# Gate rows behind the first score gather, a change of bank roles before the v products, and a later third band set in group 2: a fused attention and gMLP kernel

## The chip, the cores and the metric

The kernel runs on one core of one Trainium2 chip. The metric is device microseconds (us) of one execution, as the median of several; the profile is of one further execution. Engines: PE is the matmul engine (PEld its weight load), DVE the vector engine, ACT the scalar engine, POOL the general one, SP the engine whose queue issues nearly all transfers here. PSUM is the memory that PE writes; the kernel uses it as eight banks.

Before the change the time was 650.78 us (median of 3 runs, 650.62 to 651.17).

## The reference

The output is `g * a + (1 - g) * b`: a dilated sliding-window attention (32 heads of 32 columns, each token looks at itself and 7 earlier ones, 2 apart), a gMLP block, and a sigmoid gate per token.

```python
x = A_x                                        # 1 x 2048 x 1024
g = sigmoid((x * gate_w).sum(-1, keepdims=True))
# a: attention
qkv = x @ wqkv                                 # 1024 x 3072
logits = einsum('bhsd,bhswd->bhsw', q, k[idx]) * scale   # idx = s - 2 w, w = 0..7
o = einsum('bhsw,bhswd->bhsd', softmax(logits), v[idx])
a = o @ wo
# b: gMLP
z = gelu(x @ w_in)                             # 1024 x 3584
z1, z2 = z[..., :1792], layernorm(z[..., 1792:])
b = (z1 * (w_sp @ z2 + b_sp)) @ w_out
# ... (return g * a + (1 - g) * b; the mask for positions before the first token is left out)
```

## The kernel before

The large products are done in quads of seven block products each (a fast matrix multiplication), which trade matmuls for sums on DVE and copies on ACT. The attention works on eight groups of four heads. For each group PE computes **band sets**: small products that hold the scores of blocks of tokens against their windows. ACT evicts a set from PSUM into a slot in SBUF, the on-chip memory that the engines read (the two large sets of a group take three slots in turn), SP stores it to a buffer in DRAM, and a **gather** reads the scores of a whole group back in another layout. From there DVE takes maxima, ACT the exponential, DVE the weights, the products with v, and their sums.

```python
band_slots = [reg(R_OFF + o, 7 * BR)... for o in (30208, 32196, 38848)]
...
vq_slots = [reg(R_OFF + 39360 + 2 * VH * r, 2 * VH).bitcast(F32) for r in range(2)]
```

The third band slot starts at 38848 and is 1988 long, so it overlaps the first of the `vq_slots`, which take the **share copies** of the v quads (below). Group 2 uses the slots in the order 38848, 30208 for its two large sets (sets 2 and 3).

```python
def band_blocks(g, first, step, n, pairs=None):
    ...
        st = band_slots[band_at[0] % 3]
        band_at[0] += 1
    ...                                            # PE: the small products (L355), into banks 4 to 7
    dst = st[:, 0:n, lo:KW, :]
    src = _sub_ap(psum_all, 4 * 512 + lo, [[KW, n], [1, KW - lo], [512, HG]])
    nc.scalar.copy(dst, src)                       # ACT: eviction (L363)
    ...
        stored[id(st)].append(dma(band_free[0], 0.1 * k, lambda ...: sync.dma_start(dst, src), landed))
```

The group's interleaving with a q/k quad, and the place of the three sets:

```python
BAND_AT = (1, 3, 6)

def among_bands(g, quad):
    x = 0
    for n in range(7):
        next(quad)
        step()
        if n + 1 in (BAND_AT if g != 2 else (1, 3, 5)):
            band_set(g, x)
            x += 1
            step()
```

Each side of PSUM has four banks, whose roles X, Y, Z, V rotate from quad to quad. The start of a v quad (line numbers of the profile of before: L420, L426):

```python
bank_roles = [banks[0:4], banks[4:8]]
...
X, Y, Z, V = bank_roles[side]
...                                    # product 1 into X
nc.scalar.copy(Y[:, n], X[:, n])       # L420: the seed copy, for product 3
...                                    # product 2 into V
share(vs, V[:, n])                     # L426: the share copy, into a vq_slot
```

Group 2 is followed by the v quads, with `mark` matmuls (L558) that write two banks which the band sets have used:

```python
if g == 2:
    first = v_quad(0)
    for _ in range(2):
        next(first)
        step()
    mark(bank_roles[1][1:3], VH)
    run(v_quad(1), first, step=step)
```

DVE's work, the transfers and the exponentials are ordered by a model inside the program (`clock`, `advance`), which plays the engines forward with estimated durations and issues whatever it finds ready first. An engine then runs its instructions in that order. Its start, and the queue after the gate:

```python
T_START = (0.0, 0.0, 0.0)
...
sync.dma_start(<g_d>, g_s[:])
gate_dma = sync.dma_start(<og_d>, omg_h[:])
...
band_data[0], band_free[0], v_data[0] = T_START
clock["SP"], clock["DMA"] = 0.5, 1.5
...
next_bands()                                       # the gather of group 0's scores
dma(0.0, 0.1, lambda: sync.dma_start(g_att[:], <g_d>))
next_v(1)
```

The sums of the attention, on DVE (the lines that an experiment below edits are these):

```python
for n, ws in enumerate(...):
    yield now, ..., lambda ...: tt(a, a, b, ALU.add), not n
yield now, 1.14, lambda: tt(p3[:, 0:2, :], p3[:, 0:2, :], p3[:, 2:4, :], ALU.add), True
```

Of the kernel before, what the change touches and what calls it, by code (L numbers as in the profile page):

```python
# [13 lines left out]
P = 128  # L14
# [9 lines left out]
NJ = 16  # L24
# [34 lines left out]
def kernel(  # L59
# [34 lines left out]
    g_d = dpool.tile([S], F32, name="g_d")  # L94
    og_d = dpool.tile([S], F16, name="og_d")
# [3 lines left out]
    g_s = sm.tile([16, P], F32, name="g_s")  # L99
# [5 lines left out]
    omg_h = sm.tile([16, P], F16, name="omg_h")  # L105
    g_att = sm.tile([P, NJ], F32, name="g_att")
# [91 lines left out]
    sync = _SyncProxy()  # L198
# [3 lines left out]
    clock = dict(PE=0.0, ACT=0.0, DVE=0.0, SP=0.0, DMA=0.0)  # L202
    live = [False]
    pinned = {}
# [31 lines left out]
    def pe(dur, ready=0.0):  # L236
        return take("PE", dur, ready)
# [9 lines left out]
    def act(dur, ready):  # L247
        if live[0]:
            advance(ready)
        return take("ACT", dur, ready)  # L250
# [6 lines left out]
    def dma(ready, dur, f, landed=None, timed=False):  # L257
        if not live[0]:
            return f()
        item = [ready, dur, f, landed, timed]  # L260
        due.append(item)
        return item
# [64 lines left out]
    for i in range(4):  # L327
        vp_tile(i, middle=None)
    band_at = [0]
    last_sub = [None]  # L330
    last_evac = [None]
    BAND_SETS = [(0, 8, 2), (1, 1, 7), (9, 1, 7)]

# [1 line left out]
    stored = {}  # L335

    def band_blocks(g, first, step, n, pairs=None):
        qt, kt_ = qT_slots[g % 2], kT_slots[g % 2]
        if first == 0:
            st = band0  # L340
        else:
            st = band_slots[band_at[0] % 3]
            band_at[0] += 1
        for item in stored.get(id(st), ()):
            issue(item)
        ready = pe(T_BAND * (0.3 if n < 3 else 1.0), band_free[0])
        lo = W - 1 if first == 0 else 0
        for m in range(n):
            e, b = divmod(first + m * step, 8) if pairs is None else (m // pairs, first + m % pairs)
            for q in range(2):  # L350
                skip = lo if q == 0 else 0
                at = P * b + QB * q
                for h in range(HG):
                    hp = slice(DH * h, DH * (h + 1))
                    nc.tensor.matmul(banks[4 + h][QB * q:QB * (q + 1), m * KW + skip:(m + 1) * KW], qt[hp, e, at:at + QB],  # L355
                                     kt_[hp, e, at - (W - 1) + skip:at + QB], start=True, stop=True,
                                     tile_position=(DH * h, QB * q), skip_group_check=True)
        band_free[0] = act(0.55 if n < 3 else 1.73, ready + 0.2) + 0.15
        if lo:
            nc.scalar.copy(st[QB:P, 0:n, 0:lo, :], _sub_ap(psum_all[QB:P, :], 4 * 512, [[KW, n], [1, lo], [512, HG]]))  # L360
        dst = st[:, 0:n, lo:KW, :]
        src = _sub_ap(psum_all, 4 * 512 + lo, [[KW, n], [1, KW - lo], [512, HG]])
        nc.scalar.copy(dst, src)  # L363
        bd = band_d[g]

        def landed(t):
            band_data[g] = max(band_data[g], t)

        stored[id(st)] = []
        for q in range(2):  # L370
            for e in range(1 if pairs is None else 2):
                k = n if pairs is None else pairs
                dst = bass.AP(tensor=bd.tensor, offset=bd.offset + (2 * first + 16 * e + q) * BS, ap=[[BR, QB], [2 * step * BS, k], [1, BR]])
                src = st[QB * q:QB * (q + 1), e * k:(e + 1) * k].rearrange("p m k h -> p m (k h)")
                stored[id(st)].append(dma(band_free[0], 0.1 * k, lambda dst=dst, src=src: sync.dma_start(dst, src), landed))

    def band_set(g, x):
        band_blocks(g, *BAND_SETS[x])
# [12 lines left out]
    bank_roles = [banks[0:4], banks[4:8]]  # L391
# [4 lines left out]
    last_store = [None]  # L396
# [170 lines left out]
    def v_quad(i):  # L567
        st = vst_slots[i % 4]
        vs = vq_slots[i % 2]

        def parts(m, a, *bs):
            d = st[:, a, :].rearrange("p (g d h) -> p g d h", g=GR, h=HG)
            full = slice(3 * m, 3 * m + 2)
            at, half, hs = (0, 256, slice(0, 2)) if m == 0 else (64, 0, slice(2, 4))
            yield [d[:, full]] + [b[:, at:at + 256].rearrange("p (g h d) -> p g d h", g=2, h=HG) for b in bs]
            yield [d[:, 2, :, hs]] + [b[:, half:half + 64].rearrange("p (h d) -> p d h", h=2) for b in bs]

        for item in stored.get(id(st), ()):
            issue(item)
        stored[id(st)] = []  # L580

        def store(a):
            dv = bass.AP(tensor=v_d.tensor, offset=v_d.offset + (GP * (S + 16) + 16 + (i + 8 * a) * P) * C, ap=[[C, P], [(S + 16) * C, GR], [1, C]])
            stored[id(st)].append(dma(max(clock["ACT"], clock["DVE"]), 0.92, lambda: sync.dma_start(dv, st[:, a, :].rearrange("p (g c) -> p g c", g=GR)), v_landed))

        def put(m, a, b):
            act(0.85, clock["PE"] + 0.2)
            for dst, src in parts(m, a, b):
                nc.scalar.copy(dst, src)
            if m:  # L590
                store(a)

        def put_sum(m, a, b):
            dve(0.75, clock["PE"] + 0.2)
            insts = [nc.vector.tensor_tensor(dst, src, v, ALU.add) for dst, src, v in parts(m, a, b, vs)]
            if not m:
                store(a)
            return insts[0]

        return strassen([wvr[0][:, k, :] for k in K4], [wvr[0][:, 4 + k, :] for k in K4], [wvr[1][:, 4 + k, :] for k in K4],  # L600
                        *[[wvs[q][:, k, :] for k in K4] for q in range(4)], *x_tiles(i), vs,
                        lambda X: put(0, 0, X), lambda Z: put_sum(0, 1, Z), lambda V: put(1, 0, V), lambda Y: put_sum(1, 1, Y),
                        N=VH, flip=True, turn=False)
# [222 lines left out]
    SQH = 8  # L826
    squares = [(n, x) for n in range(16) for x in range(2)]
    LEAN = (True, True)
    T_START = (0.0, 0.0, 0.0)

    def square(n, x, junk):
        c = slice(x * HF, (x + 1) * HF)
# [48 lines left out]
# [4 lines that stand above are left out]
        for n in range(7):  # L885
            next(quad)
            step()
            if n + 1 in (BAND_AT if g != 2 else (1, 3, 5)):
                band_set(g, x)
                x += 1  # L890
                step()
        bands_have[0] = g + 1
        next(quad, 0)
# [55 lines left out]
    def step():  # L949
        advance(clock["PE"])  # L950
# [44 lines left out]
    gate_mm = nc.tensor.matmul(glT, gl_s[:], ident32[:], start=True, stop=True)  # L995
    gate_act = nc.scalar.activation(omg[:], glT, ACT.Tanh, scale=0.5)
    nc.vector.tensor_scalar(g_s[:], omg[:], 0.5, 0.5, ALU.mult, ALU.add)
    gate_vec = nc.vector.tensor_scalar(omg_h[:], omg[:], -0.5, 0.5, ALU.mult, ALU.add)
    sync.dma_start(bass.AP(tensor=g_d.tensor, offset=g_d.offset, ap=[[P, 16], [1, P]]), g_s[:])
    gate_dma = sync.dma_start(bass.AP(tensor=og_d.tensor, offset=og_d.offset, ap=[[P, 16], [1, P]]), omg_h[:])  # L1000

    settle()
    live[0] = True
    for inst in (gate_mm, gate_act, gate_vec, gate_dma):
        pinned[inst.ins.engine] = inst.ins.name
    for x in clock:
        clock[x] = 0.0
    band_data[0], band_free[0], v_data[0] = T_START
    clock["SP"], clock["DMA"] = 0.5, 1.5
    stored.clear()  # L1010
    bands_have[0] = 1
    next_bands()
    dma(0.0, 0.1, lambda: sync.dma_start(g_att[:], bass.AP(tensor=g_d.tensor, offset=g_d.offset, ap=[[NJ, P], [1, NJ]])))
    next_v(1)
    def load_wvr():
        for m in range(2):
# [8 lines left out]
    for g in range(NG):  # L1025
        main = with_quads(g, group_tiles(g))
        if g in (1, 2, 3, 4):
            load_wqk_later(g + 3, clock["PE"])
        hold[0] = g == NG - 1
        paired = play_group(g)  # L1030
        if not paired:
            play(main[0:8 - (not g)])
        if g == 2:
            first = v_quad(0)
            for _ in range(2):
                next(first)
# [3 lines that stand above are left out]
            for i in range(2, 8, 2):  # L1040
                run(v_quad(i), v_quad(i + 1), step=step)
            advance(clock["PE"] + 1.0)
            v_have[0] = NG
            next_v()
            load_later(0, clock["PE"] + 4.0, 6.0)
        if not paired:
            play(main[8 - (not g):])
# [559 lines left out]
            load_act(fp // 2 - 1)  # L1607
    out_sums_late()
    traced[0] = len(nc.cur_bb.bb.instructions)
    pinned[gate_dma.ins.engine] = last_store[0].ins.name  # L1610
    for xa in ((1, 1), (0, 1), (0, 0), (1, 0)):
        load_block(1, *xa)
    act_sums(0)
# [46 lines left out]
```

## Time and profile before

| | before |
|---|---|
| time, median | 650.78 us |
| span of the profiled execution | 648.3 us |
| PE busy | 637.5 us (98%) |
| DVE busy | 519.3 us (80%) |
| ACT busy | 298.1 us (46%) |
| granted PE clock, 200 to 250 us | 1.00 |

How to read it: a PE that is busy 98% of the span leaves 10.8 us that could be won by taking away waits.

Because the start-up differs between executions, I give positions below from the start of the gate's own matmul (L995) where I say so; it lies at 44.45 us in the profile of before.

### The profile page before, as it was taken

To read this page: it belongs to the slowest core of one execution; us is meant where nothing else is said; L and a number is where in the kernel's file an instruction comes from. 1 tells how busy PE (TensorE), PEld (TensorE's weight loads), DVE (VectorE), ACT (ScalarE), POOL (GpSimd) and SP (SyncE) were. 2 spreads that over 40 slices of the span, in tenths; PEclk is the share of its full clock that TensorE was granted. 3 is DMA by queue.
4 is the path that set the end of the run, shared out by engine and by line. 5 is a ranking of instruction groups with operands and counts; after the bars stand their busy time and mean duration, and the time that the engine had idled before them with its cause. 6 is when DMAs were issued, how large, how long until landed. Compare 5 with 4: busy or idle time off the path is not lost.

```text
span 648.3 us, 11298 instructions
## 1 busy us (share of the span) xinstructions
PE 637.5 (98%) x4345; PEld 336.2 (52%) x4391; DVE 519.3 (80%) x816; ACT 298.1 (46%) x644; POOL 15.4 (2%) x27
## 2 busy tenths in 40 slices
PE   8999999999999999999999999999999999999997
PEld 4544467444455555444444444444444444868684
DVE  0347998999899999999988766987569999586852
ACT  3547677676786878799643121121121121202120
POOL 2210000000000000001000000000000000000000
PEclk9999999999999999999999999999999999999999
DMA  9979564798687012258994578369487383557501
GB/s 218 202 162 283 115 153 103 175 226 197 133 216 201 1 51 76 66 160 233 259 257 130 130 166 189 100 202 283 91 190 174 84 158 102 107 138 127 124 28 49
DMA packets 227174, 98.19 MB, mean 151 GB/s; under 512 B 174496, under 2 KB 214064, under 8 KB 227120
## 3 DMA queue, kind: packets, MB, share of 16 engines
q1 hardware_dynamic: 226256, 95.70, 61.2%
q0 software_dynamic: 576, 1.57, 0.9%
q8 instruction: 34, 0.56, 0.4%
q10 hardware_dynamic: 288, 0.20, 0.1%
q14 instruction: 20, 0.16, 0.1%
HBM read 44.31 MB, written 36.61 MB: 125 GB/s over the span
## 4 chain that ended last, share of the span: by engine, by line
PE 90%; ACT 4%; SPq 2%; DMA 1%; DVE 1%; issue 1%; DVEq 0%; ACTq 0%
PE psum_all L402 71%; PE psum_all L1484 8%; PE psum_all L293 6%; PE psum_all L303 2%; PE psum_all L355 2%; ACT arena L838 2%; ACT arena L1175 1%; PE psum_all L790 1%; SPq L178 1%; DMA arena<-in_A_wqkv_dram 1%; SPq L194 1%; ACT arena L363 1%; ACT arena L783 1%; DMA arena<-zg_d 1%; DVE psum_all L473 0%
## 5 line engine op out<-in xcount | busy, mean ns | idle before, releaser
L402 PE MATMUL psum_all<-arena 128*128 128x512 f16 (+6 forms) x2481 | 502.5, 362 | 3.3 <-issue 0.8
L402 PEld LDWEIGHTS <-arena 128*128 128x128 f16 (+1 forms) x2518 | 244.9, 98 | 253.4 <-issue 3.2
L676 DVE TENSOR_TENSOR arena<-arena,att_A 128x2048 f16<-128x2048 bf16 x64 | 75.5, 1220 | 0.3
L473 DVE TENSOR_TENSOR psum_all<-psum_all,arena 128x512 f32<-128x512 f32 (+1 forms) x78 | 51.0, 669 | 8.7 <-PE psum_all L402 5.7
L1484 PE MATMUL psum_all<-arena 128*128 128x256 f16 (+1 forms) x468 | 51.6, 273 | 0.0
L1484 PEld LDWEIGHTS <-arena 128*128 128x128 f16 x468 | 45.8, 98 | 5.5
L293 PE MATMUL psum_all<-arena 128*128 128x512 bf16 x183 | 42.0, 379 | 1.2 <-issue 0.8
L420 ACT COPY psum_all<-psum_all 128x512 f32<-128x512 f32 (+1 forms) x24 | 12.5, 519 | 66.2 <-PE psum_all L402 65.5
L783 ACT ACTIVATE arena<-psum_all 128x448 bf16<-128x448 f32 x64 | 34.2, 545 | 18.3 <-PE psum_all L402 9.0
L1175 ACT ACTIVATE arena<-psum_all 128x512 bf16<-128x512 f32 x56 | 31.4, 613 | 19.8 <-PE psum_all L402 9.0
L680 DVE TENSOR_TENSOR arena<-arena 128x2048 f16<-128x2048 f16 x32 | 37.9, 1218 | 0.0
L363 ACT CAST arena<-psum_all 128x1988 f16<-128x1988 f32 (+3 forms) x25 | 33.9, 1358 | 2.7 <-PE psum_all L355 2.3
L838 ACT ACTIVATE arena<-arena 128x896 bf16<-128x896 bf16 x32 | 30.9, 981 | 0.0
L545 DVE TENSOR_TENSOR arena<-arena 128x512 f16<-128x512 bf16 (+5 forms) x60 | 30.1, 534 | 0.4
L444 ACT COPY psum_all<-psum_all 128x512 f32<-128x512 f32 (+1 forms) x24 | 12.3, 518 | 37.5 <-PE psum_all L402 36.8
L293 PEld LDWEIGHTS <-arena 128*128 128x128 bf16 x192 | 18.1, 98 | 21.5 <-DMA arena<-in_A_wqkv_dram 0.6
L869 ACT CAST arena<-psum_all 128x512 bf16<-128x512 f32 x40 | 22.2, 592 | 12.4 <-DVE psum_all L473 9.8
L388 DVE TENSOR_TENSOR arena<-arena 128x2048 f16<-128x2048 bf16 x8 | 9.4, 1221 | 20.9 <-DMA arena<-in_A_x_dram 20.7
L486 ACT COPY psum_all<-psum_all 128x512 f32<-128x512 f32 (+1 forms) x39 | 21.7, 570 | 6.6 <-PE psum_all L402 6.0
L426 ACT COPY arena<-psum_all 128x512 f32<-128x512 f32 (+1 forms) x24 | 12.7, 533 | 26.1 <-PE psum_all L402 22.5
L431 ACT COPY psum_all<-psum_all 128x512 f32<-128x512 f32 (+1 forms) x24 | 12.4, 517 | 25.8 <-PE psum_all L402 24.8
L549 DVE TENSOR_TENSOR arena<-arena 128x1024 f16<-128x1024 f16 (+1 forms) x16 | 11.4, 715 | 15.7 <-PE psum_all L402 15.7
(113 smaller groups left out, 530.3 us busy)
## 6 DMA issues: line engine op xcount, KB each, us to landing
arena<-v_d SPq DMA_DIRECT2D x8, 960.0 KB, 5.8
z_d<-arena SPq DMA_DIRECT2D x14, 512.0 KB, 3.9
arena<-z_d SPq DMA_DIRECT2D x14, 512.0 KB, 4.4
zg_d<-arena SPq DMA_DIRECT2D x56, 128.0 KB, 2.2
arena<-zg_d SPq DMA_DIRECT2D x32, 224.0 KB, 3.2
band_d<-arena SPq DMA_DIRECT2D x28, 248.5 KB, 4.2
arena<-in_A_wqkv_dram SPq DMA_DIRECT2D x16, 256.0 KB, 4.2
o_d<-arena SPq DMA_DIRECT2D x4, 1024.0 KB, 5.7
```

Of the source, the lines that this page charges most:

```text
L293: nc.tensor.matmul(ps[:], w[:, t, kt, :], xT[:, kt, 512 * c:512 * (c + 1)], start=(kt == 0), stop=(kt == KT - 1))
L363: nc.scalar.copy(dst, src)
L402: nc.tensor.matmul(bank[:, 0:N], lhsT, rhs, start=(start and m == 0), stop=(m == n - 1), skip_group_check=True)
L473: last_add[0] = nc.vector.tensor_tensor(out[:, n], a[:, n], vs, ALU.add)
L545: return [lambda a=a: nc.vector.tensor_tensor(*a) for a in args]
L676: lambda ws=ws, in0=in0, in1=in1: tt(p5[:, ws], in0[:, ws], in1[:, ws], ALU.mult)), False
L680: lambda a=p3[:, ws], b=p3[:, ws.start + 4:ws.stop + 4]: tt(a, a, b, ALU.add)), not n
L783: nc.scalar.activation(z2[:, i + 8 * a, ZC * c:ZC * (c + 1)], bank[:, 0:ZC], ACT.Gelu_apprx_tanh, accum_out=s1[:, 4 * n + c:4 * n + c + 1])
L838: return nc.scalar.activation(junk, src, ACT.Square, accum_out=(s2, s2h)[x][:, n:n + 1])
L869: nc.scalar.copy((qT_slots, kT_slots)[t][g % 2][:, :, 256 * (c + 2 * x):256 * (c + 2 * x + 1)], bank[:].rearrange("p (n e) -> p e n", e=2))
L1175: last_gelu[0] = nc.scalar.activation(z1s[:, f, a, :], bank[:], ACT.Gelu_apprx_tanh)
L1484: nc.tensor.matmul(bank[:, h], l, r, start=(start and m == 0), stop=(m == len(ab) - 1), skip_group_check=True)
```

## The change

Its intent: let the gather of group 0's scores go as soon as the bands are stored, not after the gate rows; make the second v product write a bank that is free earlier; and give the third band set of group 2 the same place among the steps as the other groups have. The core of the diff:

```diff
-    last_sub = [None]
+    last_band = [None]
...
+        last_band[0] = stored[id(st)][-1]
...
-    T_START = (0.0, 0.0, 0.0)
+    T_START = (-1.0, 0.0, 3.0)
...
-            if n + 1 in (BAND_AT if g != 2 else (1, 3, 5)):
+            if n + 1 in BAND_AT:
...
-    sync.dma_start(<g_d>, g_s[:])
-    gate_dma = sync.dma_start(<og_d>, omg_h[:])
...
-    for inst in (gate_mm, gate_act, gate_vec, gate_dma):
+    for inst in (gate_mm, gate_act, gate_vec, last_band[0]):
...
-    clock["SP"], clock["DMA"] = 0.5, 1.5
+    clock["SP"], clock["DMA"] = -0.5, 0.0
...
     next_bands()
-    dma(0.0, 0.1, lambda: sync.dma_start(g_att[:], <g_d>))
+    dma(0.6, 0.1, lambda: sync.dma_start(<g_d>, g_s[:]))
+    dma(0.6, 0.1, lambda: sync.dma_start(<og_d>, omg_h[:]))
+    dma(0.6, 0.1, lambda: sync.dma_start(g_att[:], <g_d>))
...
         if g == 2:
+            r = bank_roles[0]
+            bank_roles[0] = [r[0], r[3], r[2], r[1]]
             first = v_quad(0)
```

(`<g_d>` and `<og_d>` stand for the address patterns.) I call the three parts **gate**, **roles** and **slots** (the last for the place among the steps; the memory slots of the bands stay as they are).

More of the change, by code (lines that the diff above doesn't have):

```diff
@@ L998 @@
     gate_vec = nc.vector.tensor_scalar(omg_h[:], omg[:], -0.5, 0.5, ALU.mult, ALU.add)
-    sync.dma_start(bass.AP(tensor=g_d.tensor, offset=g_d.offset, ap=[[P, 16], [1, P]]), g_s[:])
-    gate_dma = sync.dma_start(bass.AP(tensor=og_d.tensor, offset=og_d.offset, ap=[[P, 16], [1, P]]), omg_h[:])
     settle()
     live[0] = True
-    for inst in (gate_mm, gate_act, gate_vec, gate_dma):
+    for inst in (gate_mm, gate_act, gate_vec, last_band[0]):
         pinned[inst.ins.engine] = inst.ins.name
@@ L1012 @@
     next_bands()
-    dma(0.0, 0.1, lambda: sync.dma_start(g_att[:], bass.AP(tensor=g_d.tensor, offset=g_d.offset, ap=[[NJ, P], [1, NJ]])))
+    dma(0.6, 0.1, lambda: sync.dma_start(bass.AP(tensor=g_d.tensor, offset=g_d.offset, ap=[[P, 16], [1, P]]), g_s[:]))
+    dma(0.6, 0.1, lambda: sync.dma_start(bass.AP(tensor=og_d.tensor, offset=og_d.offset, ap=[[P, 16], [1, P]]), omg_h[:]))
+    dma(0.6, 0.1, lambda: sync.dma_start(g_att[:], bass.AP(tensor=g_d.tensor, offset=g_d.offset, ap=[[NJ, P], [1, NJ]])))
     next_v(1)
@@ L1609 @@
     traced[0] = len(nc.cur_bb.bb.instructions)
-    pinned[gate_dma.ins.engine] = last_store[0].ins.name
+    pinned[last_store[0].ins.engine] = last_store[0].ins.name
     for xa in ((1, 1), (0, 1), (0, 0), (1, 0)):
```

## The prediction

> **What bounds the kernel now.** I read four views in this order: the busy table, the chain that ended last, the list of waits of the matmul engine (PE), and the timelines around the three places that the diff touches.
>
> ```profile
> PE 637.5 (98%) x4345; PEld 336.2 (52%) x4391; DVE 519.3 (80%) x816; ACT 298.1 (46%) x644; POOL 15.4 (2%) x27
> ...
> PE 90%; ACT 4%; SPq 2%; DMA 1%; DVE 1%; issue 1%; DVEq 0%; ACTq 0%
> ```
>
> PE is busy 637.5 of 648.3 us and is 90% of the chain. A busy PE need not run at its rate, so I also look at the pitch of the matmuls. In a stretch that holds only products 448 columns wide, the table by stretches gives:
>
> ```profile
> 200.00:250.00 50.00, 50.00 (x266) 25.86 (x265) 48.55 (x71) 38.99 (x110) 0.00 (x0) 1.00 0.29 81
> ```
>
> That is 50.00/266 = 188 ns each, at the full granted clock: no hidden waiting. Going through the start-to-start distances of all matmuls gives the same for 512 columns (215 ns), apart from lost records, which show as two pitches. So PE is at its rate nearly everywhere, and the change can win only what PE still waits for inside the touched stages. Those waits are few:
>
> ```profile
> ...
> PE psum_all L402 <- issue: 0.8, 5, 0.2
> PE psum_all L355 <- ACT arena L363: 0.8, 2, 0.6
> ...
> PE psum_all L402 <- ACT arena L869: 0.4, 1, 0.4
> ...
> PE psum_all L402 <- ACT psum_all L486: 0.3, 1, 0.3
> ```
>
> L355 are the small score products (bands), L363 their eviction by ACT, L402 all large products, L869 the copy of a q/k product out of PSUM. The 0.4 us on L869 and one of the two waits on L363 lie in group 2, the only group whose third band set comes after step 5 of the interleaved quad instead of step 6, with narrow v quads (320 columns) behind it:
>
> ```profile
> 81.29 0.59 ACT L869 CAST arena<-psum_all 128x512 bf16<-128x512 f32 x1
> 81.45 0.64 PE L355 MATMUL psum_all<-arena 32*64 32x71 bf16 x56 [0.16 <-ACT arena L363]
> 82.25 2.22 PE L402 MATMUL psum_all<-arena 128*128 128x512 bf16 x11 [0.16 <-issue]
> 82.54 1.82 ACT L363 CAST arena<-psum_all 128x1988 f16<-128x1988 f32 x1
> 84.25 1.09 ACT L869 CAST arena<-psum_all 128x512 bf16<-128x512 f32 x2
> 84.90 0.70 PE L402 MATMUL psum_all<-arena 128*128 128x320 f16 x4 [0.44 <-ACT arena L869]
> 85.44 0.43 PE L558 MATMUL psum_all<-arena 128*128 128x320 bf16 x2
> ```
>
> Group 1 has the slots that group 2 is to get:
>
> ```profile
> 61.84 0.65 PE L355 MATMUL psum_all<-arena 32*64 32x71 bf16 x56
> 62.42 2.76 PE L402 MATMUL psum_all<-arena 128*128 128x512 f16 x11
> 62.78 1.83 ACT L363 CAST arena<-psum_all 128x1988 f16<-128x1988 f32 x1
> 64.48 0.62 ACT L869 CAST arena<-psum_all 128x512 bf16<-128x512 f32 x1
> 65.02 0.59 PE L558 MATMUL psum_all<-arena 128*128 128x512 bf16 x2
> ```
>
> There PE does not wait at the third set. Last, the queue ahead of the first gather of scores:
>
> ```profile
> 45.90 0.35 SPq L189 DMA_DIRECT2D g_d<-g_s  x1
> 46.35 0.37 SPq L189 DMA_DIRECT2D og_d<-omg_h  x1
> 46.82 1.29 SPq L189 DMA_DIRECT2D att_L<-band_d  x2
> ...
> 50.62 0.29 DVE L639 TENSOR_TENSOR att_m<-att_L 128x256 f16<-128x256 f16 x1 [1.93 <-DMA att_L<-band_d]
> ```
>
> **What the Trainium skill says.** "PSUM — Partial Sum Buffer", section "PSUM bank collisions raise a hardware error", says that engines are to be kept apart bank by bank with semaphores. The trace agrees: PE goes on at 84.90, some 0.06 us after the first of the two L869 copies (about 0.59 us from 84.25) frees its bank. "Perfetto Trace Analysis", "Identifying the Most-Contended Engine", warns that matmul busy share is no measure of nearness to the limit, hence the pitch above. "TensorE: Matmul & The Clock Gate", "Back-to-back issue gap", gives N/2.4 + 2.5 ns for an isolated matmul, 189 for N=448 and 216 for 512; the trace has 188 and 215 (the faster sustained figure on that page is not seen here). "DMA: Bandwidth & Descriptors", in the anatomy of one DMA, puts about 2 us of fixed time mostly into completion; the 8 KB store of the gate landed 2.2 us after its issue.
>
> **Part 1, the gate rows behind the gather.** The two stores wait for the gate's vector operations, so the SP queue stands from 43.18 (the last band store's issue) to 45.90 and the gather of group 0's scores comes at 46.82. The last recorded landing of a band store is 44.71. The gather can then start at about 44.8, that is 46.82 - 44.8 = 2.0 us sooner, and DVE's L639 near 50.62 - 2.0 = 48.6; DVE is free from 48.69, so its 1.93 us of waiting goes. The gate rows come to some 46.1 and 46.5, their read-back into g_att to 48.4 instead of 48.16; its first reader (L655) runs at 55.41, so that is hidden. The model in the program that orders the queues also gets a later time for the v data (3.0), which I work through by its rules as placing the load of the v weights (1.3 MB) ahead of the first v gather (0.98 MB). Both went at about 0.34 MB/us before (v landed at 53.88, the weights at 57.74, 3.86 us later), so I estimate the weights at 55.0 and v at 58. DVE does the sums of the weights first and the products of group 0 some 2 us later. The amount of DVE work is the same. PE waits for nothing on DVE between 44 and 78, with 2.6 us (three products of 0.86) between an add and its use. **Worth on the path: 0.0, give or take 0.2.**
>
> **Part 2, the roles of the banks.** The second v product now writes a bank whose last reader is the eviction of step 5, not of step 6. Before, that takes away the wait of 0.44 (84.46 to 84.90). After the change of part 3 the eviction of step 6 runs ahead of the large band eviction on ACT, as in group 1 (two L869 copies, then L363), and that bank would be free either way. So parts 2 and 3 **cannot be added**.
>
> **Part 3, the third set after step 6.** Carry group 1 over by the second set's start (58.57 there, 78.81 here: +20.24):
> - third set starts at 61.84 + 20.24 = 82.08; its 56 matmuls take 0.58, to 82.66;
> - step 7 of the quad, 4 x 0.215 = 0.86, to 83.52;
> - v products 1 and 2, each 4 x 0.134 = 0.53, to 84.58;
> - then the marks (L558), which write banks 5 and 6, read by the band eviction: 62.78 + 1.83 + 20.24 = 84.85, plus 0.06: 84.91.
>
> So PE has a **new wait** of 84.91 - 84.58 = 0.33, since two narrow products fill less time than group 1's wide ones. Before, the marks start at 85.44. Gain: 85.44 - 84.91 = **0.53 us**. In waits: removed are 0.16 (ahead of the set), 0.16 (behind it) and 0.44; added is 0.33; that leaves 0.43, and the rest is pitch modelled as busy beside them. The next need is the seed copy for step 3 of the first v quad: ACT takes L869 at 84.72 for 0.6, then 0.43, ready near 85.7; PE reaches it at 84.91 + 0.27 + 0.53 = 85.71. That just fits. The share copy still waits for the store of the second set (86.14), which no part moves; step 5, which needs the copy behind it (ready 87.5), comes at 84.91 + 0.27 + 5 x 0.533 = 87.84. PE is then at its pitch to 177, so the gain stays. Sum: 0.0 + 0.53, less a little for the tight fit: 0.5 us, and 650.78 - 0.5 = 650.28, rounded to **650.3**.
>
> **Rivals.** (a) *Swallowed later*: PE waits 0.61 at 178.64 (band eviction) and 0.27 at 259.09 (a seed copy behind ACT's activations). If ACT or DVE set the pace there, the 0.5 us comes back as longer waits: 650.8. Against it: at 250.60 DVE itself waits 0.61 for PE, so it moves with PE. (b) *The new wait eats all*: a band eviction or seed copy 0.5 us later than in group 1 (ACT also runs exponentials here) makes the marks wait 0.8: 650.8. For it: the fit is tight. (c) *DVE stalls in order*: if the weights land well after 55, the sums block the adds that PE needs, by perhaps 0.5 to 1 us: 651.3. Against it: 2.6 us of slack. (d) *The new order helps*: DVE's earlier start makes the waits at 178, 259 and 291 (some 1 us with their pitch) shrink: 649.6. I see no mechanism that aims at them, only reshuffling.
>
> **Range and chances.** The runs before spread by 0.55 us. The arithmetic gives -0.5, reshuffled orders on ACT and DVE some 0.4 either way, so 649.6 to 650.9. A change of 2% is 13 us, more than all PE idle time (648.3 - 637.5 = 10.8), so faster by that is out; slower by that would need a stall of a size that the kernel has nowhere.
>
> **What would show it.** Right: the waits ahead of and behind the third set and on L869 gone, the marks at about 84.9 behind a wait of about 0.3 on L363, L639 near 48.6, PE 0.5 us ahead at 116 and still at 291. Wrong: PE idle on DVE between 50 and 66; the marks not earlier than 85.4; the lead gone after 178 or 259; or a gain above 1 us, which would have to come from waits outside the three places.

## More of the kernel before

The stage after the groups computes the second half of `x @ w_in`, in the **z2 quads**. Their sums are on DVE too (L473), in one order with the attention.

## The result, and the profile after

| | before | changed |
|---|---|---|
| time, median (range, 4 runs each) | 650.97 us (650.62 to 652.18) | 650.76 us (650.56 to 652.09) |
| ratio, 95% | | 0.9998 (0.9979 to 1.0017) |
| span of the profiled execution | 648.3 us | 649.2 us |

A ratio here is the mean time of one kernel's runs over that of the other's of the same rounds, so it is not quite the ratio of the medians. Executions over 1.5% slower than the fastest of the same kernel are left out of the means. The interval is 2.5 us wide, so it neither shows nor excludes a gain of 0.5 us. The profiled execution of the changed kernel was even 0.8 us longer. The traces have to say why.

The page of the changed kernel, its busy line and the line of its chain by engine:

```profile
PE 638.1 (98%) x4346; PEld 336.4 (52%) x4391; DVE 519.3 (80%) x816; ACT 297.8 (46%) x644; POOL 15.4 (2%) x27
...
PE 84%; ACT 4%; DVE 4%; DMA 4%; SPq 2%; issue 2%; ACTq 0%; DVEq 0%
```

Busy times are nearly unchanged. The chain is not: 4% of it are now DVE and 4% transfers, 1% each before. PE's rate in the stretch from 200 to 250 us is again 50.00 us for 266 matmuls at a clock of 1.00. Two of the new waits of PE, from its list of waits (total, times, longest):

```profile
PE psum_all L403 <- DVE psum_all L474: 0.3, 1, 0.3
PE psum_all L403 <- ACT psum_all L421: 0.3, 1, 0.3
```

(Lines have moved by one to three: L559 was L558, L403 was L402, L421 was L420, L427 was L426, L474 was L473, L640 was L639.) The wait of 0.4 us on L869 and one of the two on L363 of before are gone, as intended. New are a wait of 0.3 us of the marks on the third eviction, which was predicted, and the two shown, on a DVE addition and on a seed copy, which were not. Three places in the timeline show what happened.

**Place 1: the start of the attention.** The SP queue and DVE (start, duration, engine, operation; the idle time ahead and its cause in brackets):

```profile
44.59 3.06 SPq L189 DMA_DIRECT2D att_L<-band_d  x2
...
49.66 0.29 DVE L640 TENSOR_TENSOR att_m<-att_L 128x256 f16<-128x256 f16 x1 [0.92 <-DMA att_L<-band_d]
```

The gather is now ahead of the gate rows (whose first store goes at 47.69), but its two halves took 3.06 us to issue, since the second half waits for the last band store, whose landing is recorded at 47.09. DVE starts at 49.66 instead of 50.62.

**Place 2: group 2 and the v quads.** Before, the share copy:

```profile
86.14 0.43 ACT L426 COPY arena<-psum_all 128x320 f32<-128x320 f32 x1 [0.46 <-DMA band_d<-arena]
```

Changed:

```profile
81.32 0.63 ACT L631 ACTIVATE att_L<-att_L 128x512 f16<-128x512 f16 x1
...
85.17 0.43 PE L559 MATMUL psum_all<-arena 128*128 128x320 bf16 x2 [0.35 <-ACT arena L363]
87.23 0.43 ACT L427 COPY arena<-psum_all 128x320 f32<-128x320 f32 x1 [1.29 <-DMA band_d<-arena]
...
88.03 4.24 PE L403 MATMUL psum_all<-arena 128*128 128x320 f16 x30 [0.25 <-ACT psum_all L421]
```

An exponential (L631) now stands among the copies, the third eviction starts at 83.28, and the marks run at 85.17 instead of 85.44. Then ACT, which works in order, stands for 1.29 us with the share copy: that copy overwrites the slot of band set 2, whose store was issued at 82.07 and landed at 87.13 (before: issued at 82.04, landed at 86.04). In both, one packet of another DMA queue went by while this store was under way. The list of queues for 80 to 90 us has this line in both kernels (packets, MB, share):

```profile
q8 instruction: 1, 0.02, 0.6%
```

It comes back below. The seed copy behind the share copy, of the second v quad, comes late, and PE loses 0.41 us (from the start-to-start distances, less the pitch). The lead of 0.27 (0.32 from the gate's matmul) has become a loss.

**Place 3: group 5's scores and the z2 quads.** Before:

```profile
168.56 0.29 DVE L639 TENSOR_TENSOR att_m<-att_L 128x256 f16<-128x256 f16 x1 [2.17 <-DMA att_L<-band_d]
...
188.03 1.16 DVE L473 TENSOR_TENSOR psum_all<-psum_all,arena 128x448 f32<-128x448 f32 x2
```

Changed:

```profile
169.40 0.29 DVE L640 TENSOR_TENSOR att_m<-att_L 128x256 f16<-128x256 f16 x1 [2.88 <-DMA att_L<-band_d]
...
188.88 1.16 DVE L474 TENSOR_TENSOR psum_all<-psum_all,arena 128x448 f32<-128x448 f32 x2
```

DVE stands over 2 us for group 5's scores in both. From there to the first additions of the z2 quads it is 19.47 us before and 19.48 after: DVE has no idle time in between, and the additions come when its backlog allows, 0.85 us later than before. PE then waits for them.

### The profile page after: what moved, and what is told of

Its sections match the earlier page's. It is cut to its first block, busy times and chain, and to the rows that moved or that the text cites. A ratio compares the mean times of both kernels' runs of the same rounds, so it can differ in the third digit from the quotient of the medians.

```text
span 649.2 us, 11298 instructions
## 1 busy us (share of the span) xinstructions
PE 638.1 (98%) x4346; PEld 336.4 (52%) x4391; DVE 519.3 (80%) x816; ACT 297.8 (46%) x644; POOL 15.4 (2%) x27
## 4 chain that ended last, share of the span: by engine, by line
PE 84%; ACT 4%; DVE 4%; DMA 4%; SPq 2%; issue 2%; ACTq 0%; DVEq 0%
PE psum_all L403 69%; PE psum_all L1487 8%; PE psum_all L293 4%; PE psum_all L303 2%; DMA band_d<-arena 2%; ACT arena L839 2%; PE psum_all L355 1%; DVE arena L677 1%; ACT arena L1178 1%; SPq L189 1%; DVE arena L681 1%; SPq L178 1%; DMA arena<-in_A_wqkv_dram 1%; SPq L194 1%; DVE psum_all L474 1%
## 5 line engine op out<-in xcount | busy, mean ns | idle before, releaser
L403 PE MATMUL psum_all<-arena 128*128 128x512 f16 (+6 forms) x2482 | 503.0, 362 | 3.4 <-issue 0.6
L403 PEld LDWEIGHTS <-arena 128*128 128x128 f16 (+1 forms) x2518 | 245.1, 98 | 253.8 <-issue 4.0
L474 DVE TENSOR_TENSOR psum_all<-psum_all,arena 128x512 f32<-128x512 f32 (+1 forms) x78 | 51.0, 669 | 10.1 <-PE psum_all L403 8.3
L421 ACT COPY psum_all<-psum_all 128x512 f32<-128x512 f32 (+1 forms) x24 | 12.5, 521 | 66.8 <-PE psum_all L403 66.2
L363 ACT CAST arena<-psum_all 128x1988 f16<-128x1988 f32 (+3 forms) x25 | 34.0, 1360 | 3.6 <-PE psum_all L355 3.4
L445 ACT COPY psum_all<-psum_all 128x512 f32<-128x512 f32 (+1 forms) x24 | 12.4, 519 | 37.2 <-PE psum_all L403 36.6
L427 ACT COPY arena<-psum_all 128x512 f32<-128x512 f32 (+1 forms) x24 | 12.7, 534 | 26.3 <-PE psum_all L403 22.5
```

Of the source, the lines that this page charges most:

```text
L403: nc.tensor.matmul(bank[:, 0:N], lhsT, rhs, start=(start and m == 0), stop=(m == n - 1), skip_group_check=True)
L474: last_add[0] = nc.vector.tensor_tensor(out[:, n], a[:, n], vs, ALU.add)
```

## The experiments

**What was to be told apart.** My theory after this reading: (A) the 0.53 us of the slots part is real, but is eaten in group 2 by the share copy, which waits for a store that the change does not move; and whatever lead remains is overruled near 190 us by DVE's backlog (the work in its order that it has not yet done), whose start is set by the landing of group 5's scores. Rivals: (B) one part of the change costs by itself what another wins; (C) the profiled executions differ by chance and the kernels are alike.

The table collects what each trace showed, all in us from the start of the gate's matmul. Columns: DVE's first operation on group 0's scores; the marks of group 2; the first band set of group 3 (PE's lead after group 2 is the difference to before's 71.56); DVE's first operation on group 5's scores; the marks at the end of the z2 quads; and that last time less the one ahead of it.

| kernel | group 0 | marks, group 2 | group 3 | group 5 on DVE | end of z2 | end less group 5 |
|---|---|---|---|---|---|---|
| before | 6.17 | 40.99 | 71.56 | 124.11 | 218.77 | 94.66 |
| before_third | 6.52 | 40.98 | 72.16 | 125.60 | 220.27 | 94.67 |
| changed | 5.16 | 40.67 | 71.65 | 124.90 | 219.57 | 94.67 |
| after_again | 5.55 | 40.68 | 71.65 | 124.62 | 219.28 | 94.66 |
| slots_only | 6.17 | 40.45 | 71.69 | 124.43 | 219.08 | 94.65 |
| roles_only | 6.12 | 40.41 | 71.10 | 124.33 | 218.97 | 94.64 |
| gate_only | 4.31 | 41.21 | 71.78 | 124.53 | 219.20 | 94.67 |
| band_spare | 6.24 | 40.45 | 71.02 | 124.24 | 218.91 | 94.67 |
| dve_less | 4.33 | 40.68 | 71.76 | 125.71 | 219.12 | 93.41 |
| v_late | 6.21 | 40.39 | 71.18 | 121.95 | 219.65 | 97.70 |
| both_spare_late | 6.12 | 40.45 | 71.02 | 121.93 | 220.63 | 98.71 |
| spare_v10 | 6.12 | 40.45 | 71.02 | 121.45 | 218.86 | 97.41 |
| spare_v124 | 6.13 | 40.45 | 71.03 | 121.45 | 219.53 | 98.07 |

From the end of the z2 quads to the end of the program it is 384.8 to 385.2 us in all of them but after_again (385.64) and band_spare (385.78), which I did not trace further.

### Both kernels again

No edit; both kernels were sent once more, with the two parts below, on one chip.

> The kernel before, unchanged, as the yardstick of noise. Ratio 1.000 within 0.001. In its trace group 2 repeats: PE waits near 81.3 (0.16, band eviction), 82.1 (0.16) and 84.5 (0.44, a q/k copy), the marks at 85.4, group 3's first band set at 116.0. If DMA landings alone made the difference of 0.85 us between the two first profiles after 166 us (gather of group 6 awaited 2.17 there, 2.88 here), this repeat will have another value of that wait, anywhere from 1.5 to 3.5 us, and PE waits near 189 and 192 us may come in the kernel before too. If the change made it, the wait is 2.2 again and PE has no wait there.

> The whole change again. Ratio 0.999 to 1.001. Noise theory: the marks at 85.2 and the lost lead at 87.5 (share copy held by a band store until about 87.2) may vary by 1 us with the landing of that store; the waits at 189 and 192 us (0.43 and 0.31 in pitch) come or not. Theory that the change itself makes them: share copy again held to 87.2 within 0.2, waits at 189 and 192 again.

Measured: before 651.03 us (median of the five fast runs; the sixth is the stretched one below), changed 650.90 us (6 runs), against 651.3 us for the shared runs of before; ratios 1.0 (0.9982 to 1.0019) and 0.9999 (0.9981 to 1.0017). The profiled execution of before was a stretched one: 2386.4 us, with matmuls some 0.84 us apart at a recorded clock of 1.0. PE was slow in it and DVE hardly: DVE was busy 533.5 us, against 519.3 in the first trace. It is of no use for the comparison, and why it was so stays open. The trace of the changed kernel repeated the first one: marks at 40.68 (40.67 before), group 3 at 71.65 (71.65), share copy waiting 1.28 us. So group 2 of the changed kernel is reproducible, and its marks are 0.3 us sooner than before's, its group 3 no sooner. The scores of group 5 came 0.28 us sooner than in the first trace and the z2 quads ended 0.29 us sooner.

### The slots part alone

```diff
-            if n + 1 in (BAND_AT if g != 2 else (1, 3, 5)):
+            if n + 1 in BAND_AT:
```

> Only the third band set of group 2 moved from behind step 5 to behind step 6; gate stores and bank roles as before. If the prediction's step for this part holds, the waits of 0.16, 0.16 and 0.44 go, the marks wait some 0.3 on the band eviction and start near 84.9 (0.5 us sooner than 85.44). If the exponential that stands behind the second eviction in the changed kernel comes with this part, the marks start at 85.1 to 85.2 and the gain is 0.3. Roles have no part in it: the second v product does not wait in either case. Total: within 0.1% of before.

Measured: 651.38 us (6 runs), ratio 0.9995 (0.9979 to 1.001). The marks ran 0.54 us sooner (40.45 for 40.99), which is the predicted 0.53. Then:

```profile
88.92 0.43 ACT L426 COPY arena<-psum_all 128x320 f32<-128x320 f32 x1 [1.54 <-DMA band_d<-arena]
89.72 0.57 PE L402 MATMUL psum_all<-arena 128*128 128x320 f16 x3 [0.51 <-ACT psum_all L420]
```

The share copy waits 1.54 us for the store of set 2, and PE loses 0.67 us on the seed copy behind it. Group 3 begins 0.13 us later than before. The first half of theory A holds: the gain is made, and lost 3 us later.

### The roles part alone

```diff
+            r = bank_roles[0]
+            bank_roles[0] = [r[0], r[3], r[2], r[1]]
             first = v_quad(0)
```

> Only the swap of two bank roles ahead of the v quads; third set still behind step 5. Expected by the prediction's working: the wait of 0.44 ahead of the second v product goes (PE reaches it at 84.46 and its bank was emptied at 82.6), the marks follow at 85.0 without a wait, because the eviction ended at 84.36: 0.44 us sooner than before, nearly as much as the moved set. Rival: the seed copy of step 3 now comes later than needed and gives it back, so the step 3 product starts no sooner than before (86.25).

Measured: 651.34 us (6 runs), ratio 1.0 (0.9983 to 1.0017). PE goes from the q/k products into the v products and the marks without a wait:

```profile
82.05 2.99 PE L402 MATMUL psum_all<-arena 128*128 128x512 bf16 x16
```

Its marks come 0.58 us sooner, and group 3 begins 0.46 us sooner. The removed wait is 0.44 in the view and 0.60 in start-to-start distances less the pitch (the end of a matmul is modelled, and hides the rest); 0.12 of the lead is gone again by group 3, of which 0.09 behind the share copy, which waits 0.96 us here. This part keeps its lead through group 2 in this trace. Yet its z2 quads ended at 218.97, not sooner than before's 218.77: PE lost 0.70 us there (in two places, 0.39 and 0.31). Group 5's scores had come 14.63 us after the group's third band set, before 13.95.

### The gate part alone

The diff above without its slots and roles parts.

> Only part 1: the gate rows stored behind the first gather, with the new start times of the ordering model; group 2 as before. Theory now: the group 2 waits (0.16, 0.16, 0.44) all stay and the marks start within 0.1 of 40.99 us after the gate matmul; L640 (first attention op of group 0) starts about 1 us sooner (5.2 to 5.6 instead of 6.17), but DVE idles for scores of group 5 anyway (first op at 124.3 to 124.9 after the gate matmul, with 2 to 3 us of waiting before it), so the lead of DVE is worth nothing at the end. The prediction's 2.0 us for L640 needs the last band store to land by 44.8; rival, seen in the changed kernel: it lands near 47, the second half of the gather waits for it.

Measured: 650.35 us (one run).

```profile
84.93 0.70 PE L403 MATMUL psum_all<-arena 128*128 128x320 f16 x4 [0.68 <-ACT arena L870]
```

Here the last band store landed early, and DVE starts at 48.57, as predicted for the whole. But the part costs something in group 2: PE waits 0.68 us for the copy of a q/k product where before it waited 0.44. The cause, read from the trace and not tested by itself, stands in ACT's order. In the kernels with this part the exponential of group 1 (L631, 0.63 us) lies behind the second band eviction, as the line at 81.32 of the changed kernel showed; in before it runs ahead of that eviction, in time that ACT otherwise idles (0.74 us in gate_only):

```profile
78.71 0.64 ACT L630 ACTIVATE att_L<-att_L 128x512 f16<-128x512 f16 x1
```

The part also moves group 1's maxima, on which the exponential works: DVE begins them 33.32 us after the gate's matmul instead of 32.21. Group 3 begins 0.22 us later. So rival B holds in small: this part costs 0.22 us in group 2 and returns nothing that I could find, since DVE stands still at 166 us in any case.

### A later load of v rows, to bring group 5's scores forward

On top of the roles part, the gather of group 4's v rows (0.98 MB on the same queue) is issued later, by 14.0 in the ordering model.

```diff
-            dma(max(clock["DVE"] + 0.1 if gone[0] else 0.0, v_data[0]), 2.75, ...
+            dma(max(clock["DVE"] + 0.1 if gone[0] else 0.0, v_data[0]) + (14.0 if h == 4 else 0.0), 2.75, ...
```

> Roles swapped as in the run of that part alone, and the gather of group 4's v rows (0.98 MB) issued behind the gather of group 5's scores instead of ahead of the stores of those scores. Theory: behind 166 us DVE is saturated from the landing of group 5's scores to 190, and PE's waits in the first z2 quads are DVE's lag: loss = (start of group 5's first DVE op minus start of the z2 marks) + 14.8 us; the five profiles so far fit that within 0.03. If so, the scores now land 1 us or more sooner (first op before 123.6), PE loses nothing near 144 and 147.5 after the gate matmul, and the marks at 218.77 (best so far) come at 218.3. Rival (the loss there is ACT's or the order's own): the waits of 0.3 to 0.7 stay although the scores come sooner.

Measured: 650.59 us (one run).

```profile
180.78 0.29 DVE L639 TENSOR_TENSOR att_m<-att_L 128x256 f16<-128x256 f16 x1 [2.69 <-DMA att_L<-band_d]
```

Group 5's scores came 2.4 us sooner than in roles_only (121.95 for 124.33; DVE began on them at 166.28, after a wait of 0.42). The wait came back one group later, as the line shows: 2.69 us for group 6's scores, behind the v rows that had been put off. PE lost 0.99 and 0.31 us in the z2 quads, and they ended at 219.65 for an expected 218.3: a miss. The end is fixed by whichever scores DVE waits for last: in this kernel, in both_spare_late and in spare_v124 the end of z2 follows DVE's first operation on group 6 by 83.20 us.

### Roles and slots, with the two band slots exchanged

If the share copy's wait for set 2 is what eats the gain, then giving set 2 of group 2 another slot must keep it. The edit is the roles and slots parts, and:

```diff
-... for o in (30208, 32196, 38848)]
+... for o in (30208, 38848, 32196)]
```

> Roles and third set as changed, gate as before, and the three slots of the band tiles in another order, so that group 2's second set no longer lies where the v quads keep their shared term. Theory: the wait of the share copy (1.3 to 1.5 us on the store of that set, until 42.7 after the gate matmul) and PE's loss of 0.4 to 0.7 at 42.8 to 43.0 go; marks at 40.45 as with the moved set alone, group 3's first band set at 71.0 (before 71.56, changed 71.65). The end is still set by group 5's scores, so the z2 end marks stay at 218.7 to 219.6. Rival: the loss at 42.8 is the seed copy's own length and stays.

Measured: 651.07 us (one run).

```profile
85.70 0.46 ACT L426 COPY arena<-psum_all 128x320 f32<-128x320 f32 x1
```

The share copy runs at once, and group 3 begins 0.54 us sooner than before. Against slots_only the marks are at the same place (40.45 in both) and the loss of 0.67 us behind them is gone, although the store of set 2 landed as late as there (42.64 and 42.66 us after the gate's matmul); the share copy's wait was its cause. (Against slots_only the run has the roles part too, which touches neither the share copy's slot nor that store.) It also shows again that roles and slots do not add up: together 0.54, roles alone 0.46. And here too the lead is gone at the end of z2 (218.91 against 218.77), with group 5's scores at 14.63 us after the third band set, and PE losing 0.41 and 0.31 us in the z2 quads. The kernel was timed once only, so whether it is faster than before is not measured.

### The exchanged slots together with the later v rows

Both edits above, in the hope of a kernel that keeps the lead to the end.

> All that should pay together: roles, third set, other slot order, late gather of group 4's v rows, gate as before. If both theories hold, group 3's first set at 71.0 and the z2 end marks near 218.2 after the gate matmul, 0.5 us before the best profile of before; the total 650.3 against 650.8 to 651.3, ratio 0.999, which the interval of the runs may not resolve.

Measured: 651.81 us (6 runs), ratio 1.0016 (1.0 to 1.0032). Group 6's scores were waited for 3.70 us, and the z2 quads ended at 220.63. A miss: this is the same trade as in v_late, with a worse draw.

### The kernel before, a third time

No edit; to get an undisturbed second trace of it, and to see how much of what I read is chance.

> The kernel before once more, for the second sound trace of it that the stretched profile did not give. Group 3's first band set at 71.56 after the gate matmul within 0.05. The first DVE op of group 5 (124.11 in the first trace) may fall anywhere in 124.0 to 125.0; the marks at the end of the first z2 quads come 94.66 us after it (218.77 in the first), as they do within 0.02 in the seven traces of the undelayed kernels.

Measured: 651.83 us (one run), beside 652.33 us for before's runs on that chip.

```profile
87.88 0.43 ACT L426 COPY arena<-psum_all 128x320 f32<-128x320 f32 x1 [2.02 <-DMA band_d<-arena]
```

This changed my reading. The unchanged kernel, too, can wait 2.02 us at the share copy, when the store of set 2 lands late; it then loses 0.61 us. And its scores of group 5 came 14.85 us after the third band set, for 13.95 in the first trace, and its z2 quads ended 1.50 us later. So the first trace of before was a lucky one in both places (its execution took 650.11 us; of the 44 timed runs beside the experiments and the result one alone is shorter), and rival C is right in part: the 0.8 us by which the first two profiled spans differ need not be the change's doing, as before's own two differ by more (648.3 and 650.0). A rival to chance is the chip: this run, dve_less and spare_v10 ran on another chip than the other experiments. The median of before is the highest there, and the two longest times from the third band set to group 5's scores (14.85 and 15.36 us) are from it. No run tells chip and chance apart.

### One DVE addition less

To show that DVE's backlog sets the end of z2, one of its additions of 1.22 us between group 5's start and the z2 additions is left out of the changed kernel. The result is wrong (relative error 0.0786).

```diff
-                yield now, 1.14, lambda: tt(p3[:, 0:2, :], ...
+                yield now, 1.14, (lambda: None) if (g, e) == (3, 1) else (lambda: tt(p3[:, 0:2, :], ...
```

> The whole change, with one vector addition (1.22 us, group 3's second half, at 181 us) left out, so the result is wrong on purpose; every order is the same otherwise. Theory that DVE's backlog behind group 5's scores sets PE in the first z2 quads: PE's losses near 144.4 and 147.8 after the gate matmul (0.74 and 0.46 in sum in the two traces of the change) go to 0 to 0.2, and the distance from group 5's first DVE op to the marks at the end of the quads shrinks below 94.66, by 1.2 at most and to PE's own limit of 79.9 us behind the first marks. Rival that ACT (two table loads there) or the landing itself sets it by another way: distance stays 94.66.

Measured: 650.32 us (one run).

```profile
169.99 0.29 DVE L640 TENSOR_TENSOR att_m<-att_L 128x256 f16<-128x256 f16 x1 [3.53 <-DMA att_L<-band_d]
...
188.21 1.16 DVE L474 TENSOR_TENSOR psum_all<-psum_all,arena 128x448 f32<-128x448 f32 x2
```

From group 5's start to the additions it is now 18.22 us instead of 19.48, and from there to the end of z2 the sum in the table falls from 94.67 to 93.41: by 1.26 us for an addition that takes 1.22. PE lost only 0.19 us in the z2 quads although this trace had the latest scores of all (15.36 us after the third band set). That is what a stretch bound by DVE must do.

### Two places for the v rows between the two

The edit of both_spare_late with 10.0 and with 12.4 in place of 14.0.

> Roles, third set and other slot order as in the run before, and group 4's v gather between group 5's gather and group 6's stores. In the two runs with the gather still later, group 5's scores came 2.3 us sooner (121.9) but group 6's scores were then awaited 2.7 and 3.7 us, for the v rows went ahead of group 6's last store. Here group 6's store should land as before, its scores be awaited less than 1 us, PE lose under 0.3 near 144, and the end marks come at 218.2 to 218.5. Rival: the v rows delay group 6's stores as well, the marks come at 219 or later, and there is no place for 0.98 MB in this stretch that costs nothing.

> The last try at a kernel that keeps the lead of group 2: roles, third set and other slot order, group 4's v rows some 1.5 us earlier in the queue than in the latest two of the late runs (behind the first store of group 6 instead of between its last ones), and with the vector order that has the two adds of the first z2 quads ahead of the attention sums (in the run with the rows right behind group 5's gather a sum of 1.22 us stood ahead of them, and PE lost 0.43 there although the scores came at 121.45). Expected: group 5's first op near 121.9, group 6's about 135 after a wait of 1 to 1.5 us, PE's loss near 144 under 0.4, end marks at 218.3 to 218.7 after the gate matmul against 218.77 to 220.27 of before. The time 650.5 to 651; ratio 0.999 with an interval that holds 1. Rival: group 6's scores are awaited 2 us or more again, the end marks come at 219 or later.

Measured: with 10.0, 651.71 us (4 runs), ratio 1.0 (0.9972 to 1.0028); group 6 was waited for 1.33 us, a sum of 1.22 us slipped ahead of the z2 additions in DVE's order, and PE lost 0.43 us there and 0.26 us more than the other traces at a seed copy near the end of the z2 quads (259.75 us); z2 ended at 218.86. With 12.4, 650.83 us (6 runs) beside 651.46 for before, ratio 0.9986 (0.9968 to 1.0003); group 6 was waited for 3.08 us, z2 ended at 219.53. Neither is shown to beat the kernel before. I found no place for these 0.98 MB that costs nothing, so no better version came of it.

## Why the prediction was right or wrong

The forecast of no change by 2% and the range (649.6 to 650.9) held: 650.76 us. Luck has a part in the range: the medians of the unchanged kernel in the later calls (651.3, 651.31, 651.46, 652.33) all lie above it. The **0.5 us of gain at its centre was not shown**, and the traces say that most of it was not there. By its own steps:

- **PE at its rate, waits few: right.** The rate was 188 ns per 448-column matmul in both kernels, and all differences found are waits.
- **Part 1, mechanism right, size half missed.** The gather moved ahead, but L639 went to 49.66, not 48.6. I took the landing of the last band store in the one trace of before, 44.71, for what it would be again; in the changed kernel the store issued last landed at 47.09. In gate_only it landed at 44.98 and the number was met (48.57). The guess that the v weights would go ahead of the first v gather was wrong: the queue's order differs in the two gate stores alone. It did no harm. Its worth "0.0, give or take 0.2" was just missed: it costs 0.22 us, by way of an exponential that now stands ahead of the copies that PE waits for. That is a part of rival (b), "ACT also runs exponentials here".
- **Part 2: right, in its size partly by luck.** 0.44 predicted; alone the marks came 0.58 us sooner and group 3 0.46, as the wait was longer than the view shows and some of the lead was lost again. It does not add to part 3: together 0.54, in a kernel with the memory slots exchanged.
- **Part 3, the sum right to 0.01, the step behind it wrong.** Alone, the marks came 0.54 us sooner for a predicted 0.53. In the whole change they came 0.32 us sooner, since the exponential of part 1 put the third eviction to 83.28 for a predicted 83.02; the new wait, in start-to-start distances less the pitch, was 0.28 us alone and 0.51 in the whole change for a predicted 0.33 (the view shows 0.35 of the 0.51).
- **"The share copy still waits for the store of the second set (86.14), which no part moves": this step failed.** No part moves its issue, yet I treated its landing as a constant. It landed at 87.13, in before_third later still, and the seed copy behind the copy cost 0.41, 0.67 and 0.61 us in three kernels. I had checked the product of step 5 against its copy behind the share copy (ready 87.5, needed at 87.84). I had not checked the third product of the second v quad, one product earlier: by my times PE reaches it at 84.91 + 0.27 + 4 x 0.533 = 87.31, and its seed copy, which also stands behind the share copy, ended at 86.93 before. There was room for some 0.3 us only. With 0.32 - 0.41 = -0.09 us, group 3 of the changed kernel begins no sooner than before's. band_spare shows this to be the cause, by taking the overlap away.
- **And a part does move that landing.** In all thirteen usable traces the store is issued 37.57 to 37.60 us after the gate's matmul, and one packet of 16,384 bytes of the queue that the profile calls "instruction" (q8, the line in place 2) starts before it lands. In the eight traces of kernels with the slots part that packet starts at 39.88 to 40.08, and the store lands at 42.59 to 42.75 (seven have the landing recorded). In the five without, it starts at 38.05 to 38.24 and takes 0.93, 1.25, 1.40, 1.42 and 1.74 us, and the store lands at 41.59, 41.86, 42.08, 42.15 and 43.13, in this order. So the landing in the changed kernel repeats with the slots part, later than in four of the five traces without it; the trace of the changed kernel was no unlucky draw there. That the packet holds up the store is what the order suggests: no run tests it.
- **"PE is then at its pitch to 177, so the gain stays": wrong for what follows 177.** This is rival (a), swallowed later, at a place I had not named. I looked at PE's waits at 178 and 259 us and found them small. I did not look at DVE's one wait of 2.17 us for group 5's scores at 166 us, as DVE was not the bound. In the trace of before, PE reached the z2 additions just as DVE's backlog ended, so it shows no wait. PE needs some 79.87 us for the stretch from the first to the last z2 marks; before took 79.90, roles_only 80.56, of which it lost 0.70. In the eight traces (of six kernels) with the same order and full work the end of z2 is DVE's first operation on group 5 plus 94.64 to 94.67 us. The sums of DVE there are strictly in order, as the Trainium skill ("Perfetto Trace Analysis", "Tensor Engine Instruction (MATMUL, LD_WEIGHTS)") says of ACT and DVE, "strict FIFO" (each takes its instructions in order); the traces agree: the additions for which PE waits stand behind 19.47 and 19.48 us of other work without a gap.

So does half a microsecond of lead on PE count? If the scores always came the same time after the third band set, they would come sooner by the lead, and it would stay. Measured, that time is 13.95, 14.85, 14.65, 14.38, 14.15, 14.63, 14.15, 14.63 and 15.36 us (table order, to dve_less): a spread of 1.4 us, nearly three times the lead. On average a lead should still be worth something. That is an argument, not a measurement: the runs resolve no less than a microsecond. What makes this landing vary is open.

## What to carry to other kernels

A wait that is removed counts only as far as the next thing that did not move with it. Follow the lead on from there, and treat the landing of a transfer as a range, taken from two or three traces of the unchanged kernel; then look whether it moved with the change, even where its issue did not. Look at the one long wait of an engine that is *not* the bound, too: where it has a full backlog afterwards and the bound engine needs the end of that backlog, that wait sets the end.

## What the Trainium skill lacked or had wrong

- "TensorE: Matmul & The Clock Gate", "Back-to-back issue gap": the sustained figure for 512 columns (about 131 ns) is not seen in this kernel; its dense streams run at 215 ns, and at 188 ns for 448 columns, which is the page's formula for an isolated matmul.
- "DMA: Bandwidth & Descriptors", anatomy of one DMA: its fit (made for another issue path than this queue) would put a band store of 254,464 bytes at an estimated 2.0 + 0.58 = 2.6 us. The page of the profile has 4.2 us as the median of these stores before and 4.6 us after. One figure for a size was also too little here: the store of set 2 took 4.00 us from issue to landing before (82.04 to 86.04) and 5.06 us after (82.07 to 87.13).
